# Retention and ELU feed-forward on one core: first batch read in runs of four tokens, heads on partition halves, chunks of 256 tokens, opening reordered

## The chip, the cores and the metric

The kernel runs on one core of one Trainium2 chip. The metric is the device time of one execution in microseconds. Three runs of the kernel before took 302.07, 301.1 and 301.15 us, so its median is 301.15.

## The reference

For each of 8 batches and 8 heads, with 576 tokens and a head size of 64, the scores are weighted with a power of the distance and multiplied with v. There is no softmax. The result, with the heads side by side, is the input of a two-layer network with ELU between the layers.

```python
scores = q @ k.T / sqrt(64)
gamma  = 1 - 2 ** (-5 - h)                       # one per head
ret    = (scores * where(i >= j, gamma ** (i - j), 0)) @ v
x      = ret, as [8 * 576 tokens, 8 heads * 64]
out    = elu(x @ w_in) @ w_out                   # w_in 512 x 2048, w_out 2048 x 512
```

All arrays in HBM are float32; the kernel multiplies in bfloat16. The power splits into a factor on q and a factor on k (`gamma ** i` and `gamma ** -j`), so decay costs one scaling of q and one of k.

## The kernel before

**Items.** The 512 leading tokens of a batch are cut into four *items*: two stretches T of 256 tokens, times two groups w of four heads (L346 to L355). The last 64 tokens of the batches are two tail items at the end. An item goes through these steps:

- `load_main` (L381): three DMAs, q, k and v of the item, 256 KB each. A partition holds two neighbouring tokens of four heads, so a run in HBM is two tokens long, 512 bytes, and 128 partitions take the 256 tokens. The SP queue issues them in the order q, k, v of item 0, of item 1, and so on.
- `scaled` (L469): q and k times their factors, to bfloat16, on VectorE or GpSimd, 128x256 at a time; `cast_v` (L507): v to bfloat16 on ScalarE, VectorE or GpSimd.
- `turn_pe` (L517): TensorE turns q and k; the results are copied from PSUM to `qkT`.
- `do_scores` (L625), `mask_step` (L833): scores of k and q in chunks of 128 tokens (64 partitions, two tokens each), 16 matmuls of 64x128, then one multiplication 128x1024 with the causal mask.
- `do_state` (L722), `after_state` (L738): the product of k and v of each chunk, summed to the running states `mid` and `end`, and laid out by `block` as the block-diagonal tiles `s_mid`, `s_end`. The second chunk of an item and all later ones need a state.
- `do_inter`, `do_values` (L658, L689), `put_x` (L892): q times state plus masked scores times v, copied to `xt`, the input of the network.

The first four items, which are the first batch, go through `early` and `early_out` (L996, L1009): everything by itself, as nothing else is there to do. Later items are woven into the network in `stretch` (L939). From item 12 on (`FAR`) an item has another layout.

**The network.** `ffn1` (L1026) multiplies a block of `xt` with an eighth or sixteenth of w_in, ScalarE takes the exponential, ScalarE or VectorE the positive part, VectorE joins the two; `ffn2` (L1073) multiplies with w_out. The first two blocks are 256 tokens wide, the two halves of the first batch. The weights come in eight pieces of 512 KB after the cast to bfloat16 (1 MB in HBM), issued from GpSimd's queue (`load_w_in`, `load_w_out`, L450, L460).

**What sets the order.** All steps are given to a planner (`Plan`, L37 to L191) as operations with a cost per engine, dependencies, a rank and the buffers they take. It simulates the engines and DMA queues, and at each step gives the free engine the ready operation of lowest rank. The instructions are then issued in the order that comes out (L1203 to L1224), and each engine takes its own in that order. `FROM` (L208) holds the times, in the planner's clock, from which the weight pieces may be issued; `HOLD` (L198) ties the load of item 4 to the landing of the first weight piece; `ON` (L209) fixes the engine of some steps; `RANKS` (L199) shifts ranks and is empty. Where the planner leaves TensorE idle in the first 50 us, matmuls on zeros fill the gap (L1213 to L1222), and ten 128x512 ones go ahead of everything (L1143).

Factors and masks are built before the planned part: the positions by `iota` on GpSimd, the exponents on VectorE, the factors by three exponentials on ScalarE (L1147).

Of the kernel before, what the change touches and what calls it, by code (L numbers as in the profile page):

```python
# [36 lines left out]
class Plan:  # L37
# [30 lines left out]
    def run(self, began):  # L68
# [58 lines left out]
        while len(order) < len(self.ops) or any(wire.values()) or events:  # L127
# [53 lines left out]
            for e, h in heads.items():  # L181
                h[1] -= step * rate[e]
                if h[1] < 1e-6:
                    wire[e].pop(0)
                    lanes[e] -= 1
                    heapq.heappush(events, (now + LEAVE, next(count), h[2]))
# [7 lines left out]
ENTER, LEAVE = 1.25, 0.55  # L194


LEAD = 64
HOLD = {4: "wi0"}  # L198
RANKS = {}  # L199
# [8 lines left out]
FROM = (8.96, 10.28, 13.13, 15.23, 17.0, 17.0, 17.44, 17.82)  # L208
ON = {'mid1': 'DVE', 'be2': 'DVE', 'md_1_0': 'ACT', 'xc1_2': 'DVE', 'cv0': 'DVE', 'md_1_1': 'ACT', 'cq12': 'DVE'}  # L209
DIRECT = True  # L210
# [5 lines left out]
TWO = False  # L216
# [6 lines left out]
FREE = ("f", "e", "g", "ot")  # L223
# [4 lines left out]
    "rqk": 7, "rv": 6, "qkn": 5, "vn": 6, "qkT": 5, "pt": 3,  # L228
    "rqt": 2, "rvt": 2, "qkt": 2, "vt": 4, "qkTt": 8,
    "xt": 3, "g": 28, "e": 4, "ot": 5, "mid": 6, "end": 4, "s_mid": 8, "s_end": 18,  # L230
# [4 lines left out]
def kernel(  # L235
# [44 lines left out]
    lgt = const.tile([P, H], FP32, name="lgt")  # L280
    for h in range(H):
        nc.vector.memset(lgt[:, h : h + 1], lg[h])
    pos_i = const.tile([P, NU], I32, name="pos_i")
    nc.gpsimd.iota(pos_i[:, :FT].rearrange("p (t e) -> p t e", e=2), pattern=[[2 * P, 2], [1, 2]], base=-MID,
                   channel_multiplier=2)
    nc.gpsimd.iota(pos_i[:ST, FT:], pattern=[[0, 1]], base=FT * P - MID, channel_multiplier=1)
    nc.gpsimd.iota(pos_i[ST:, FT:], pattern=[[0, 1]], base=MID - FT * P, channel_multiplier=-1)
    pos = const.tile([P, NU], FP32, name="pos")
    nc.vector.tensor_copy(pos, pos_i)
# [4 lines left out]
    bt = const.tile([P, 1], FP32, name="bt")  # L294
    nc.vector.memset(bt[:ST], math.log(scale))
    nc.vector.memset(bt[ST:], 0.0)
    expo = const.tile([P, NU, H], FP32, name="expo")
    nc.vector.tensor_tensor(
        expo,
        pos.unsqueeze(2).to_broadcast([P, NU, H]),  # L300
        lgt.unsqueeze(1).to_broadcast([P, NU, H]),
        ALU.mult,
    )
    gq = const.tile([P, NU, H], FP32, name="gq")
# [7 lines left out]

    mask = const.tile([P, 2, 2, C], BF16, name="mask")
    nc.vector.memset(mask, 1.0)
    for c in range(2):
        m = mask[c * C : (c + 1) * C]
        nc.gpsimd.affine_select(out=m, in_=m, compare_op=ALU.is_ge, fill=0.0, base=0,
                                pattern=[[-1, 2], [1, 2], [2, C]], channel_multiplier=-2)
    mask_t = const.tile([P, ST], BF16, name="mask_t")
    nc.vector.memset(mask_t, 1.0)  # L320
# [3 lines left out]
    nc.vector.memset(diag[D:, 1:], 1.0)  # L324

# [45 lines left out]
    for n, it in enumerate(items):  # L371
        it.n = n
        it.early = n < FT
        it.far = n >= FAR and not it.tail
        it.xt = xt_of(it.blk)
        it.rank = n * 4 - 64 if it.early else base[it.blk] - LEAD + (
            16 * it.t if it.tail else 6 * it.w + (SPREAD * it.T if width[it.blk] > TB else 0))
# [3 lines left out]
    def load_main(it, srcs="qkv"):  # L381
        n = it.n
        if not hasattr(it, "ld"):
            it.ld = {}
        for s in srcs:
# [3 lines left out]
            away = (s, n) in AWAY  # L389

# [59 lines left out]
    def load_w_in(n0, n1, after):  # L450
        c = slice(n0 * 512, n1 * 512)

        def emit(op):
            pin(nc.gpsimd.dma_start(w_in_sb[:, :, c], moe_w_in[:, c].rearrange("(j p) n -> p j n", p=P)))  # L454

        op = add(f"wi{n0}", {"POOL": 0.8}, [], emit, -1000, dma=(2.62 * (n1 - n0), 32 * (n1 - n0), 4.9), after=after)
        for n in range(n0, n1):
            w_in_ld[n] = op

    def load_w_out(n, after):  # L460
        def emit(op):
            pin(nc.gpsimd.dma_start(w_out_sb[:, 4 * n : 4 * n + 4],
                                    moe_w_out[n * 512 : (n + 1) * 512, :].rearrange("(f p) n -> p f n", p=P)))

        w_out_ld[n] = add(f"wo{n}", {"POOL": 0.8}, [], emit, -1000, dma=(2.62, 32, 4.9), after=after)

    def scaled(it, i, e, cost):  # L469
        n = it.n  # L470
        key, raw = ("qkn", n), ("rq" + "qk"[i], n)
# [3 lines left out]
        def emit(op):  # L475
            pin(alu[op.eng].tensor_tensor(tiles[key][:, i, e], tiles[raw][:, :, e], g, ALU.mult))  # L476
# [4 lines left out]
        ready = [it.ld["qk"[i], e], far_ready[0]] if it.far else [it.ld["qk"[i]]]  # L481
# [25 lines left out]
    def cast_v(it, cost):  # L507
        n = it.n

        def emit(op):  # L510
            pin(copy[op.eng](tiles["vn", n], tiles["rv", n]))  # L511

        ready = [it.ld["v", 0], it.ld["v", 1]] if it.far else [it.ld["v"]]
        it.cv = add(f"cv{n}", cost, ready, emit, it.rank, take=[T("vn", ("vn", n), [P, 4, 2, D], BF16)],
                    use=[("rv", n)])
# [52 lines left out]
    def prepare_tail(it):  # L568
# [3 lines left out]
        for m in range(2):  # L572
            for j in range(2):
                parts = []
                for h in range(2):
                    hs = slice(h * 4, h * 4 + 4)

                    def emit(op, m=m, j=j, hs=hs):
# [4 lines left out]
                                     [it.ld[0, m, j], it.ld[1, m, j]], emit, it.rank,  # L583
# [74 lines left out]
    def do_inter(it, xkey, o=0):  # L658
        n = it.n
        if it.tail:  # L660
            for m in range(2):
                for j in range(2):
                    for hp in range(HP):
                        s = tiles["s_end", 4 * it.t + 2 * m + j, 1, hp // 2]
                        o = (m * HP + hp) * ST
                        acc((xkey, j), 0, 2, tiles[xkey, j][:, o : o + ST], s[:, hp % 2],
                            tiles["qkTt", n, m, j][:, hp, :ST])
# [12 lines left out]
        for c in range(2):  # L680
            if it.T + c == 0:
                continue
            for name in ("s_end", "s_mid") if c and it.two else ("s_mid",) if c else ("s_end",):
# [54 lines left out]
    def after_state(it, st, views, bank_keys):  # L738
# [24 lines left out]
        def block(src, key, name, dep):  # L763
# [7 lines left out]
            return add(name, {"POOL": 0.62, "DVE": (0.42, 0.4 if it.early else 1.5)}, [dep], emit, it.rank + 3,  # L771
                       take=[T(key[0], key, [P, 2, P], BF16)], use=[src])

        it.two = TWO and it.early and it.T == 1
        if it.two or (DIRECT and it.early and it.T == 0):
            key = ("s_mid", it.b, it.T, it.w)

            def emit_bm(op):
                pin(nc.vector.tensor_tensor(
                    tiles[key].rearrange("p h (j d) -> p h j d", j=2),  # L780
                    st_ap(0).unsqueeze(2).to_broadcast([P, 2, 2, D]),
                    diag.unsqueeze(1).unsqueeze(3).to_broadcast([P, 2, 2, D]), ALU.mult,
                ))

            it.bm = add(f"bm{n}", {"DVE": 0.43}, [st], emit_bm, it.rank + 1, take=[T("s_mid", key, [P, 2, P], BF16)],
                        use=[views[0][0]], banks=[bank_keys[0]])
        else:
            it.bm = block(("mid", n), ("s_mid", it.b, it.T, it.w), f"bm{n}", mid)
# [44 lines left out]
    def mask_step(it, sc):  # L833
# [24 lines left out]
        it.mask = add(f"mask{n}", {"DVE": 0.69 if it.far and it.two_of is None else 1.22}, [sc], emit, it.rank + 1,  # L858
# [57 lines left out]
    def cost_of(it, parts):  # L916
# [3 lines left out]
        if "i" in parts:  # L920
            t += 0.056 * (16 if it.tail else 6 if it.two else 4 if it.T else 2)
# [73 lines left out]

    def early(it):  # L996
        n = it.n
# [11 lines left out]
    def early_out(it):  # L1009
        n = it.n  # L1010
# [109 lines left out]

    far_ready = [add("far_i", {"POOL": 0.2}, [], emit_far_i, 0)]
# [4 lines left out]
    for it in items:  # L1126
# [8 lines left out]
    def emit_mask_t(op):  # L1135
        for c in range(2):
            m = mask_t[c * ST : (c + 1) * ST]
            pin(nc.gpsimd.affine_select(out=m, in_=m, compare_op=ALU.is_ge, fill=0.0, base=0, pattern=[[1, ST]],
# [4 lines left out]
    def emit_warm(op):  # L1143
        for _ in range(10):
            mm(tiles["warm"], zero[:, :P], zero, start=True, stop=True)

    def emit_factors(op):  # L1147
        pin(nc.scalar.activation(gq[:, :FT], expo[:, :FT], AF.Exp, bias=bq))
        pin(nc.scalar.activation(gk, expo[:, :FT], AF.Exp, bias=bk, scale=-1.0))
        pin(nc.scalar.activation(gq[:, FT], expo[:, FT], AF.Exp, bias=bt))  # L1150

    add("factors", {"ACT": 0.8}, [], emit_factors, -10 ** 6).at = 2.8
    add("warm", {"PE": 3.0}, [], emit_warm, -10 ** 6, take=[T("f", "warm", [P, 512], FP32)])
# [17 lines left out]
    for i, blk in enumerate(seq):  # L1171
# [3 lines left out]
        rank = base[blk] + width[blk] // 16 + 1  # L1175
# [18 lines left out]
    for n, t in enumerate(FROM):  # L1194
        named[f"{'wi' if n < 4 else 'wo'}{n % 4}"].at = t
        if n % 4:
            named[f"{'wi' if n < 4 else 'wo'}{n % 4}"].turn.append(named[f"{'wi' if n < 4 else 'wo'}{n % 4 - 1}"])
    named["wo0"].turn.append(named["wi3"])
    for name, e in ON.items():
        named[name].cost = {e: named[name].cost[e]}  # L1200
    for name, shift in RANKS.items():
        named[name].rank += shift
# [6 lines left out]
    for op in order:  # L1209
        for cls, key, shape, dt in op.take:  # L1210
            pool = psum if cls in ("f", "sc") else sbuf
            tiles[key] = pool.tile(shape, dt, name=cls, tag=f"{cls}{op.slot[key]}")
        if op.eng == "PE":  # L1213
            gap = op.start - last if op.start < 50 and op.take else 0.0
            if gap > 0:
                spot = tiles[op.take[0][1]]
                for n in range(int(gap * 0.8 / 0.056)):
                    if op.name.startswith("T"):
                        pin(nc.tensor.transpose(spot[:, n % 4], zero[:, :P], ident))
                    else:  # L1220
                        mm((spot if len(spot.shape) == 2 else spot[:, 0])[:, :P], zero[:, :P], zero[:, :P],
                           start=True, stop=True)  # L1222
# [35 lines left out]
```

## Time and profile before

| | us |
|---|---|
| median of three runs | 301.15 |
| the profiled execution | 301.8 |
| its span, first to last instruction | 300.1 |
| TensorE busy in the span | 291.5 |
| ScalarE, VectorE, GpSimd busy | 188.2, 172.3, 164.4 |
| first matmul on weights starts | 19.06 |
| twelve loads of the first batch, first and last landing | 3.72, 15.95 |
| eight weight pieces, first and last landing | 18.00, 40.06 |

The profile is of one execution; its span leaves out what lies around the first and last instruction, here 1.7 us. The granted clock of TensorE is 1.0 over the whole span. In the lists below, PE is TensorE's matmul, PEld its weight load, ACT is ScalarE, DVE VectorE, POOL GpSimd, and SP the engine that issues most DMAs. In a timeline a row has its start, its length, the engine, the line of the kernel, the operation, the tile written and the tiles read, and in brackets how long the engine was idle before and for whom it waited. In a table by windows a row has the stretch, its length, the busy time and number of instructions of PE, PEld, DVE, ACT and POOL, the granted clock, the share of the DMA engines' time and the rate in GB/s.

### The profile page before, as it was taken

To read this page: it belongs to the slowest core of one execution; us is meant where nothing else is said; L and a number is where in the kernel's file an instruction comes from. 1 tells how busy PE (TensorE), PEld (TensorE's weight loads), DVE (VectorE), ACT (ScalarE), POOL (GpSimd) and SP (SyncE) were. 2 spreads that over 40 slices of the span, in tenths; PEclk is the share of its full clock that TensorE was granted. 3 is DMA by queue.
4 is the path that set the end of the run, shared out by engine and by line. 5 is a ranking of instruction groups with operands and counts; after the bars stand their busy time and mean duration, and the time that the engine had idled before them with its cause. 6 is when DMAs were issued, how large, how long until landed. Compare 5 with 4: busy or idle time off the path is not lost.

```text
span 300.1 us, 8496 instructions
## 1 busy us (share of the span) xinstructions
PE 291.5 (97%) x3367; PEld 169.5 (56%) x3402; DVE 172.3 (57%) x312; ACT 188.2 (63%) x365; POOL 164.4 (55%) x292
## 2 busy tenths in 40 slices
PE   8899999999999999999999999999999999999996
PEld 4678746768767764545544554554545444444444
DVE  4888934948865537696843675646442474334300
ACT  2439724838766656786776667676764686777611
POOL 5790389984988849598794888579330000000000
DMA  6999999999998998999999999976761101011132
GB/s 201 272 207 210 226 292 316 231 260 184 179 238 183 217 205 193 219 191 212 192 224 165 173 231 208 186 176 106 175 142 72 35 0 38 35 35 37 35 106 70
DMA packets 135607, 50.10 MB, mean 167 GB/s; under 512 B 108176, under 2 KB 131088, under 8 KB 135568
## 3 DMA queue, kind: packets, MB, share of 16 engines
q1 hardware_dynamic: 131344, 45.37, 71.0%
q0 software_dynamic: 4224, 4.19, 8.4%
q8 instruction: 26, 0.43, 0.6%
q14 instruction: 13, 0.11, 0.1%
HBM read 36.70 MB, written 9.44 MB: 154 GB/s over the span
## 4 chain that ended last, share of the span: by engine, by line
PE 92%; DMA 2%; SPq 2%; issue 1%; POOL 1%; DVE 0%; ACT 0%; ACTq 0%
PE f L269 89%; PE sc L269 3%; DMA rqk<-in_q_dram 2%; SPq L405 2%; POOL qkn L476 1%; PE f L524 1%; POOL w_in_sb L454 0%; DVE xt L907 0%; ACT ot L1094 0%; ACTq L1094 0%
## 5 line engine op out<-in xcount | busy, mean ns | idle before, releaser
L1060 DVE SCALAR_TENSOR_TENSOR g<-e,f 128x512 bf16<-128x512 f32 x144 | 96.3, 685 | 79.3 <-ACT f L1053 78.7
L269 PE MATMUL f<-w_out_sb,g 128*128 128x512 bf16 (+2 forms) x582 | 136.9, 367 | 2.7 <-issue 1.9
L269 PE MATMUL f<-xt,w_in_sb 128*128 128x256 bf16 (+1 forms) x759 | 138.8, 325 | 0.6 <-DVE xt L907 0.2
L1045 ACT ACTIVATE e<-f 128x512 f32<-128x512 f32 x144 | 85.4, 596 | 48.0 <-PE f L269 41.6
L269 PEld LDWEIGHTS <-w_in_sb 128*128 128x128 bf16 x768 | 74.1, 98 | 53.2 <-DVE xt L907 0.5
L269 PEld LDWEIGHTS <-g 128*128 128x128 bf16 x608 | 56.7, 98 | 58.3
L1053 ACT ACTIVATE f<-f 128x512 f32<-128x512 f32 x122 | 72.2, 593 | 0.0
L818 POOL TENSOR_TENSOR s_mid<-mid,diag 128x256 bf16<-128x256 f32 x60 | 35.6, 613 | 12.9 <-DVE mid L807 7.9
L1094 ACT COPY ot<-f 128x512 f32<-128x512 f32 (+2 forms) x38 | 21.4, 566 | 22.6 <-PE f L269 22.6
L476 POOL TENSOR_TENSOR qkn<-rqk,far_q 128x256 bf16<-128x256 f32 x40 | 23.8, 613 | 5.5 <-DMA rqk<-in_q_dram 5.4
L476 POOL TENSOR_TENSOR qkn<-rqk,far_k 128x256 bf16<-128x256 f32 x40 | 23.9, 613 | 0.4 <-DMA rqk<-in_k_dram 0.2
L511 POOL CAST vn<-rv 128x512 bf16<-128x512 f32 x28 | 17.0, 610 | 7.3 <-DMA rv<-in_v_dram 7.3
L476 POOL TENSOR_TENSOR qkn<-rqk,gq 128x256 bf16<-128x256 f32 x21 | 13.1, 635 | 12.1 <-DMA rqk<-in_q_dram 12.1
L907 ACT CAST xt<-f 128x256 bf16<-128x256 f32 x24 | 9.2, 425 | 14.1 <-PE f L269 14.1
L851 DVE TENSOR_TENSOR pt<-sc,mask 128x1024 bf16<-128x1024 f32 x12 | 14.6, 1219 | 4.3 <-PE sc L269 4.2
L845 DVE TENSOR_TENSOR pt<-sc,mask_t 128x1024 bf16<-128x1024 f32 (+1 forms) x12 | 12.5, 1042 | 5.7 <-PE sc L269 4.2
L1055 DVE TENSOR_SCALAR f<-f 128x512 f32<-128x512 f32 x22 | 15.2, 695 | 0.9 <-ACT e L1045 0.6
L579 POOL TENSOR_TENSOR qkt<-rqt,gq 128x256 bf16<-128x256 f32 x16 | 9.5, 613 | 10.6 <-DMA rqt<-in_k_dram 10.6
L883 ACT CAST xt<-f 128x512 bf16<-128x512 f32 x16 | 8.6, 589 | 10.2 <-PE f L269 9.5
L476 POOL TENSOR_TENSOR qkn<-rqk,gk 128x256 bf16<-128x256 f32 x22 | 13.3, 621 | 2.4 <-DMA rqk<-in_k_dram 2.4
L818 POOL TENSOR_TENSOR s_end<-end,diag 128x256 bf16<-128x256 f32 x20 | 12.3, 613 | 0.4 <-DVE end L807 0.3
L807 DVE TENSOR_TENSOR mid<-f,mid 128x256 f32<-128x256 f32 (+1 forms) x24 | 9.1, 380 | 2.5
(81 smaller groups left out, 170.7 us busy)
## 6 DMA issues: line engine op xcount, KB each, us to landing
out_dram<-ot SPq DMA_DIRECT2D x30, 256.0 KB, 3.0
rqk<-in_q_dram SPq DMA_DIRECT2D x40, 128.0 KB, 3.4
rqk<-in_k_dram SPq DMA_DIRECT2D x40, 128.0 KB, 3.3
rv<-in_v_dram SPq DMA_DIRECT2D x40, 128.0 KB, 3.1
rqk<-in_q_dram SPq DMA_DIRECT2D x12, 256.0 KB, 5.8
rqk<-in_k_dram SPq DMA_DIRECT2D x12, 256.0 KB, 5.4
rv<-in_v_dram SPq DMA_DIRECT2D x12, 256.0 KB, 6.9
w_in_sb<-in_moe_w_in_dram POOLq DMA_DIRECT2D x4, 512.0 KB, 8.8
```

The lines of the kernel that those rows point to most:

```text
L269: pin(nc.tensor.matmul(*a, **kw))
L476: pin(alu[op.eng].tensor_tensor(tiles[key][:, i, e], tiles[raw][:, :, e], g, ALU.mult))
L511: pin(copy[op.eng](tiles["vn", n], tiles["rv", n]))
L579: pin(alu[op.eng].tensor_tensor(tiles["qkt", n, m, j][:, hs], tiles["rqt", n, m, j][:, hs], g[:, hs], ALU.mult))
L818: pin(alu[op.eng].tensor_tensor(tiles[out].rearrange("p h (j d) -> p h j d", j=2), tiles[key][:, i].unsqueeze(2).to_broadcast([P, 2, 2, D] ...
L845: pin(nc.vector.tensor_tensor(tiles[it.pt].rearrange("p i h n -> p (i h n)")[:, : 2 * w * C].rearrange("p (i x n) -> p i x n", i=2, n=C), ...
L851: pin(nc.vector.tensor_tensor(tiles["pt", n].rearrange("p i h n -> p (i h) n"), tiles[it.sc].rearrange("p i (h n) -> p (i h) n", h=2), mas ...
L1045: pin(nc.scalar.activation(tiles[ekey], tiles[hkey], AF.Exp))
L1053: pin(nc.scalar.activation(ph, ph, AF.Relu))
L1055: pin(nc.vector.tensor_scalar_max(ph, ph, 0.0))
L1060: pin(nc.vector.scalar_tensor_tensor(tiles[gkey], tiles[ekey], -1.0, tiles[hkey], ALU.add, ALU.min))
L1094: pin(copy[op.eng](tiles[okey][:, :cols], tiles[pkey][:, :cols]))
```

## The change

The first batch gets a path of its own; all later items compute what they did. The diff is cut to the core.

**Loads.** A tensor of 256 tokens and all eight heads is read into one tile by two DMAs, of heads 0 to 3 into partitions 0 to 63 and of heads 4 to 7 into partitions 64 to 127. A partition holds four neighbouring tokens, so a run is 1 KB. There are again twelve DMAs of 256 KB, in the order q, k of tokens 0 to 255, q, k of tokens 256 to 511, v of 0 to 255, v of 256 to 511. An item is now two heads of each half. The four tiles of q and k lie in the place of w_out.

```diff
+            if it.early:
+                raw = ("r8" + s, it.T)
+                for g in range(2):
+                    def emit_quad(op, src=src, raw=raw, g=g):
+                        pin(nc.sync.dma_start(
+                            tiles[raw][g * ST : (g + 1) * ST],
+                            src[it.b, 4 * g : 4 * g + 4, 2 * P * it.T : 2 * P * (it.T + 1), :].rearrange(
+                                "h (p e) d -> p h (e d)", e=4)))
+SEQ = 'q0 k0 q2 k2 v0 v2'
+    for word in SEQ.split():
+        load_main(items[int(word[1])], word[0])
...
+            if cls == "r8" and op.slot[key] < 4:
+                n = op.slot[key] * 4
+                tiles[key] = w_out_sb[:, n : n + 4].bitcast(FP32)...
```

**Chunks of 256 tokens.** `quad` takes the place of `early` and `early_out` for the first four items. The scores of all 256 tokens are computed in two halves of eight matmuls of 64x256, into four banks; the mask is four multiplications 128x512 per item instead of one of 128x1024. There is no state inside a stretch. The value step has 16 matmuls of 64x256, with 16 of 64x64 that build the state in the same bank; for tokens 256 to 511 the latter are done anew for both stretches (32), and two matmuls of 128x256 bring in the state of the first. One copy per item goes to `xt`, one step (`be`) lays out the state. The accumulator of the value step takes the one slot of the class `sc`, so the next item's value step waits for both copies.

```diff
+            sc = add(f"sc{n}_{half}", {"PE": 0.33}, it.turned, emit_sc, it.rank + half, use=[("qkT", n)])
...
+        xv = add(f"iv{n}", {"PE": 0.85 + 0.33 * len(olds)}, [*it.masks, it.cv] + [u.be for u in olds], emit_x, it.rank + 3,
+                 take=[T("sc", xkey, [P, 2, 512], FP32)],
```

**Constants.** The factors and the mask of the first batch are new and small, and are built first. Those of the later items (`near_l`, `near_i`, `near_x`, `near_f`, `mask_n`) become planned operations, and the later scalings and masks wait for them.

**The order.** Costs in the planner change (`QUAD_LD`, `PIECE`), landings in a stretch of its clock get 1.5 us more (`LAG`), eight warm-up matmuls stand for ten, and the fillers use 128x512 matmuls where a gap is long. The load of item 4 is tied to the last w_in piece. `RANKS` and `ON` get long lists, and the second product of the first two blocks a lower rank.

```diff
-HOLD = {4: "wi0"}
-RANKS = {}
+HOLD = {4: 'wi3'}
+RANKS = {'T(5, 0)': 8, 'iv2': -2, 'xc_1': -2, ...}
-FROM = (8.96, 10.28, 13.13, 15.23, 17.0, 17.0, 17.44, 17.82)
+FROM = (5.3, 4.0, 11.5, 8.4, 4.0, 20.1, 7.4, 17.9)
+QUAD_LD = 0.67
+F2_RANK = -16
```

What comes out, by engine, in the opening:

- SP: the twelve loads, then the loads of item 4 on.
- POOL: masks and memsets, one scaling of the first q, three iotas, w_in pieces 0 and 1, eight scalings, w_in pieces 2 and 3, w_out piece 0, the later constants, the other w_out pieces.
- DVE: seven scalings, the later exponents, one copy of turned q and k, then the masks one after another, between them a copy of turned k, one positive part and one copy to `xt`.
- ACT: the factors, three copies of turned q and k, the later factors, a copy, the casts of v of items 0 and 1, a copy, the copy to `xt` of item 0, the cast of v of item 2, the state of item 0 (two copies), the cast of v of item 3, a copy, the copy to `xt` and the state of item 1, then the exponentials.
- PE: warm-up, turns and scores of items 0 and 1, the turns of item 2, the value step of item 0, the scores of item 2, the turns of item 3, the value step of item 1, the scores of item 3, one first product, the value step of item 2, three first products, the value step of item 3, and from there products.

## The prediction

> **What bounds the kernel now.** The head of the page comes first.
>
> ```profile
> span 300.1 us, 8496 instructions
> ## 1 busy us (share of the span) xinstructions
> PE 291.5 (97%) x3367; PEld 169.5 (56%) x3402; DVE 172.3 (57%) x312; ACT 188.2 (63%) x365; POOL 164.4 (55%) x292
> ```
>
> TensorE works nearly all the time. Next is its timeline, to see where it does not.
>
> ```profile
> 14.77 0.56 PE L524 MATMUL f<-ident,qkn 128*128 128x128 bf16 x4 [1.00 <-DVE end L757]
> ...
> 19.06 1.05 PE L269 MATMUL f<-xt,w_in_sb 128*128 128x256 bf16 x8
> ...
> 20.61 1.38 PE L269 MATMUL f<-xt,w_in_sb 128*128 128x256 bf16 x11
> 22.19 8.03 PE L269 MATMUL f<-xt,w_in_sb 128*128 128x256 bf16 x72 [0.21 <-DVE xt L907]
> ```
>
> From 22.19 on it runs through; no later wait in this view is over 0.2 us. So the time is the opening plus a fixed amount of TensorE work. A matmul of the first FFN product costs 0.11 us (72 in 8.03), and 19 of them are done before 22.19, so the FFN starts in effect at 22.19 - 19 x 0.11 = **20.1 us**. This net start is what I follow: one microsecond on it is one on the time. The chain of waits for the first 25 us says what sets it.
>
> ```profile
> 6.33 0.67 SPq L405
> 7.00 0.04 issue
> 7.04 7.02 DMA rqk<-in_q_dram
> 14.06 0.07 issue
> 14.13 0.85 POOL qkn L476
> ...
> 18.39 3.28 PE f L269 x57
> ```
>
> The opening is a chain of loads: the fourth q, issued at 7.04, lands at 14.06. By the trace's landing records the twelve 256-KB loads land at 3.72, 4.55, 6.31 and then every 0.9 us to 11.81; the last three at 14.06, 14.86 and 15.95. So the question is what the new loads do. Three kinds of transfer stand side by side in the table by windows; the last two columns are the DMA engines' share and GB/s.
>
> ```profile
> 8.00:12.00 4.00, 3.89 (x96) 3.18 (x94) 4.00 (x10) 1.72 (x5) 3.96 (x7) 1.00 1.17 292
> 26.00:31.00 5.00, 5.00 (x48) 4.47 (x47) 4.45 (x8) 4.80 (x10) 0.69 (x2) 1.00 1.19 214
> 278.40:279.80 1.40, 1.40 (x9) 0.62 (x7) 0.69 (x1) 0.76 (x3) 0.00 (x0) 1.00 0.83 186
> 288.30:289.10 0.80, 0.80 (x6) 0.35 (x4) 0.00 (x0) 0.00 (x0) 0.00 (x0) 1.00 0.86 328
> ```
>
> The first is the old loads, 128 partitions, runs of 512 B. The second is loads against weight pieces. The third is 256 KB of output stored as two halves of 64 partitions, the fourth the same bytes in one store of 128: 186 against 328 GB/s, with runs of 2 KB in both. In the packet records a packet of the halves takes 153 ns at the median, one of the whole store 85.
>
> **The change, step by step. 1. The loads.** Twelve loads of 256 KB stay, but each now has 64 partitions and runs of 1 KB, in the order q, k of tokens 0-255, q, k of 256-511, then both v. No row shows a 1-KB load or a load of 256 KB on 64 partitions, so I bound it. From below: eight packets of 84 ns per engine, 0.67 us, the packet time of the whole store; 1 KB between the rows of 512 B (28 ns) and 2 KB (84) would be 46 ns x 16 = 0.74. From above: the halves of the store, 1.41 us for 256 KB with start and end, or 8 x 153 ns = 1.22 in a row of loads. I take 1.22, for the row with the same partitions is the nearest, and keep 0.67 to 1.41. The two halves of a tensor follow each other on the same queue, as the halved stores do.
>
> The Trainium skill has a rule on this: SBUF — State Buffer says in its section "Door 1: The DMA port swizzle" that a transfer on partitions 0-63 reaches half of the 16 ports, and in "Can I just issue two DMAs to hit both halves?" that two, one on each half, gain 6% over one. Its 196 GB/s for 64 partitions would make 1.34 us of a half-load (an estimate from that page) and the sum below 1.0 us longer; the 186 of the trace's stores agrees with it, but no run here shows it for loads.
>
> With data from 2.0 (first window above 100 GB/s) and landing 0.75 after the last byte (3.72 = 2.0 + 0.9 + 0.8; 4.55 likewise), q of the first half lands at 2.0 + 2 x 1.22 + 0.75 = 5.2, against 3.72 for half as much data before.
>
> **2. The weights join.** On POOL the first w_in piece now stands behind one scaling (0.85, as at 14.13) that waits for this q, and three iotas (0.13 each): issued at 5.2 + 0.85 + 0.4 = 6.45, the second right behind. Before, issue was at 9.08, and the rate fell from 292 to 245 GB/s at 13.0, 4 us later. So weights join at 10.45, when (10.45 - 2.0)/1.22 = 6.9 half-loads are in. In the stretch 26-31 loads and weights pass packet for packet: load and weight landings both come every 3.65 us (30.17, 33.82, 37.47; 29.04, 32.75, 36.34), with 512 packets each. A half-load has 256, so 1.83 us. The two pieces last 7.3 us, to 17.75; four half-loads pass. k of tokens 256-511 (8th) ends at 12.4, lands at 13.15; v of 0-255 (10th) 16.05 and 16.8; the rest alone, 1.07 x 1.22: the last v lands at **19.8**, against 15.95.
>
> **3. What stands behind the casts of v.** ACT takes its work in order. After the change it is: cast v (items 0, 1), a copy of the transposed k, xc_0, cast v (item 2), two state copies, cast v (item 3), a copy of transposed q, xc_1. The starts of ACT's rows give what one costs in a queue:
>
> ```profile
> 9.19 0.58 ACT L530 COPY qkT<-f 128x512 bf16<-128x512 bf16 x1 [1.13 <-PE f L524]
> 9.67 0.62 ACT L511 CAST vn<-rv 128x512 bf16<-128x512 f32 x1
> 10.19 0.45 ACT L907 CAST xt<-f 128x256 bf16<-128x256 f32 x1
> ```
>
> 0.5 each; a 128x128 copy 0.27, so two 0.5. From 16.8: cast, then the first value product 17.45 to 18.3, xc_0 to 19.1, idle to 19.8, cast to 20.3, states to 20.85 (they free the one accumulator, so the second value product runs 20.95 to 21.75), cast 21.4, copy 21.9, xc_1 to 22.6. TensorE does item 3's scores meanwhile and starts the first FFN product at **22.75**, three matmul groups behind a chain that before had none of v in it.
>
> **4. TensorE's own work.** Sixteen 64x64 matmuls take 0.25 us to the next start, sixteen of 64x128 0.35; 256 columns then 0.35 + 0.2 = 0.55. A value step of tokens 256-511 is 0.55, two rounds of states 0.5, and two 128x256 at 0.11: 1.27. Both of these still come after 22.75, so the net start is 22.75 + 2.54 = **25.3**, and the change costs 25.3 - 20.1 = **5.2 us**.
>
> **5. What I cost at nothing.** Masks: 16 of 128x512, half of the 1.22 of 128x1024, 9.8 us on DVE instead of 4.9; with the last v at 19.8 they lie in the wait for it, and if v comes early they are late next (rival 2). The constants of the later batches move to POOL and ACT in the opening, under a microsecond each, covered by the same wait; the new waits on them are met 10 us before use. Eight warm-up matmuls for ten, fewer fillers: idle time either way. Raw q and k lie in w_out's place, so those pieces wait for scalings over by 17; wo0 follows w_in by 10 us, before its first use. Loads of item 4 held for wi3 instead of wi0, and the shifts of rank and engine later: after 22 us TensorE alone binds; 0.3 either way.
>
> **How it could go.** *Forecast, halves at half rate*: 301.15 + 5.2 = 306.4 us. The sum is made on a profiled execution of span 300.1, which itself took 301.8, 0.65 above the median; it would take 307.0. With 1.41 the same steps give 21.3 for the last v and +6.7, 307.9. For it: the third row above, and weights that join before the loads are done.
>
> *Rival 1, halves that overlap in part*: before, the sixteen parts of a load land up to 1.3 us apart, so engines out of step would fill both halves at once. With 1.0 us a half-load the same steps land v at 18.1, +3.5: 304.7. Against it: the two halves of a store show no such gain (186 GB/s over both).
>
> *Rival 2, no loss from halves, and faster*: it decides below about 0.8 us a half-load. At 0.67 weights join at 9.35 with 11 of 12 in, the last v lands at 12.0, and DVE binds: first mask at 8.0 (k at 5.4, four scalings 1.4, turn, copy, scores 1.2), 16 x 0.61 and 1.7 of others to 19.5, last value product to 21.0 with 3.5 us of FFN already done: 17.5, so -2.6, 298.5. At 0.74 v lands at 13.7, -0.9, 300.2; at 0.82 at 15.3, +0.7, 301.8. For it: half the packets, the old loads at 292 GB/s were below the 328 that longer runs show.
>
> *Late parts*: q at 14.06 was held by one of sixteen parts 1.5 us behind the others (12.51); if this hits the last v, each case is up to 1.5 later. TensorE would wait over 3 us for v; its first ten 128x512 matmuls took 0.43 each against 0.22 later. A fall back to that pace after the wait costs up to 1.5; I add neither, but the top of the range has them.
>
> **Numbers.** Forecast 0.52, rival 1 0.15, rival 2 0.33 (of it 0.25 clearly faster, 0.07 no change, 0.01 slower). A measurement here tells 0.3% (0.9 us) from no change: faster 0.25, same 0.07, slower 0.68. Likeliest case 304.9 to 308.4; the range that leaves out 2 in 10, 298.8 to 308.4.
>
> **What would show it.** Right: in the first 10 us windows near 215 GB/s where 292 stood; DVE's or POOL's first scaling after 5 us; ACT idle before a cast of v up to about 20; the FFN stream from about 23. Wrong: windows above 330 GB/s, the last v before 14, or DVE with no gap between masks: then rival 2.

## The result, and the profile after

The kernel after took **308.77 us** (median of four runs, 307.85 to 309.81) against 301.12 for the kernel before: 1.025 times as long, 95% interval 1.021 to 1.029, or 7.65 us more. The forecast was 306.4, so the direction is right and the size 2.4 us short. The range ended at 308.4 and missed the time by 0.4 us.

The profiled execution took 309.8, some 1.0 above the median; its span is 308.1, 8.0 more than the profiled one of before. First the head of its page.

```profile
span 308.1 us, 8508 instructions
## 1 busy us (share of the span) xinstructions
PE 297.9 (97%) x3379; PEld 171.3 (56%) x3379; DVE 175.2 (57%) x308; ACT 197.5 (64%) x382; POOL 160.5 (52%) x299
```

The shares look as before. The difference is in the first 32 us, and the table by windows has it (granted clock, share of the DMA engines' time and GB/s are the last three columns).

```profile
5.00:10.00 5.00, 3.57 (x30) 2.50 (x29) 3.23 (x9) 1.73 (x4) 2.80 (x6) 1.00 1.11 216
10.00:15.00 5.00, 3.50 (x59) 2.30 (x56) 4.10 (x7) 1.28 (x5) 3.12 (x6) 1.00 1.16 219
15.00:20.00 5.00, 3.65 (x65) 2.77 (x64) 2.87 (x5) 2.83 (x4) 4.88 (x9) 0.74 1.19 238
20.00:25.00 5.00, 3.12 (x55) 2.40 (x56) 1.45 (x3) 3.90 (x8) 3.10 (x9) 0.50 1.24 206
25.00:30.00 5.00, 5.00 (x76) 3.84 (x75) 3.65 (x6) 1.93 (x5) 0.00 (x0) 0.74 1.21 212
30.00:35.00 5.00, 5.00 (x88) 4.28 (x86) 3.67 (x9) 4.82 (x11) 0.61 (x1) 1.00 1.20 215
```

Two things are to be seen. Where the loads stand alone, up to 13.8, when the first packet of a weight piece is moved, they move at 216 to 219 GB/s (292 before), with the DMA engines busy all the time. And the granted clock, 1.0 throughout before, is at half from 17.4 to 27.6 us by the clock records. The chain of waits in order of time (start, length, what) names what it hangs on:

```profile
8.22 12.47 DMA r<-in_v_dram
...
20.77 0.62 ACT vn L552
21.39 0.16 ACT blocks L1109
...
21.88 1.28 PE sc L275 x20
23.16 3.47 PE f L275 x29
```

The last load, v of tokens 256 to 511, lands at 20.70 by the landing records; the casts and state copies follow on ScalarE, then TensorE. TensorE's timeline shows what the clock does to the steps:

```profile
19.36 0.63 PE L568 MATMUL f<-ident,qkn 128*128 128x128 bf16 x4
21.88 1.07 PE L275 MATMUL sc<-pt,vn 64*64 64x256 bf16 x16 [1.88 <-ACT blocks L1109]
...
23.74 1.07 PE L275 MATMUL f<-qkT 64*64 64x256 bf16 x16
24.74 1.89 PE L275 MATMUL f<-xt,w_in_sb 128*128 128x256 bf16 x8
26.42 0.64 PE L275 MATMUL sc<-qkT,blocks 128*128 128x256 bf16 x2
...
28.10 2.79 PE L275 MATMUL f<-xt,w_in_sb 128*128 128x256 bf16 x24
...
31.86 2.31 PE L275 MATMUL f<-xt,w_in_sb 128*128 128x256 bf16 x19
```

The first product (eight matmuls) takes 1.89 here and took 1.05 before. From 31.86 the stream runs through, with 32 products of 0.11 done: the net start is 31.86 - 3.5 = **28.35**, against 20.1 before. That is 8.25 later, and the span is 8.0 longer: nearly all of the loss lies in the opening.

### The profile page after: what moved, and what is told of

The parts are those of the page before. It is cut to its first block, busy times and chain, and to the rows that moved or that the text cites. A ratio compares the mean times of both kernels' runs of the same rounds, so it can differ in the third digit from the quotient of the medians.

```text
span 308.1 us, 8508 instructions
## 1 busy us (share of the span) xinstructions
PE 297.9 (97%) x3379; PEld 171.3 (56%) x3379; DVE 175.2 (57%) x308; ACT 197.5 (64%) x382; POOL 160.5 (52%) x299
## 4 chain that ended last, share of the span: by engine, by line
PE 92%; DMA 4%; SPq 2%; ACT 0%; issue 0%; ACTq 0%
PE f L275 88%; DMA r<-in_v_dram 4%; PE sc L275 4%; SPq L407 2%; PE f L568 0%; ACT vn L552 0%; ACT blocks L1109 0%; ACT ot L1220 0%; ACTq L1220 0%; ACTq L552 0%
## 5 line engine op out<-in xcount | busy, mean ns | idle before, releaser
L275 PE MATMUL f<-w_out_sb,g 128*128 128x512 bf16 (+2 forms) x608 | 143.0, 368 | 0.0
L275 PE MATMUL f<-xt,w_in_sb 128*128 128x256 bf16 (+1 forms) x768 | 142.1, 327 | 0.0
L555 POOL CAST vn<-rv 128x512 bf16<-128x512 f32 x26 | 15.8, 610 | 8.2 <-DMA rv<-in_v_dram 8.1
L516 POOL TENSOR_TENSOR qkn<-rqk,gq 128x256 bf16<-128x256 f32 x14 | 8.5, 613 | 19.1 <-DMA rqk<-in_q_dram 19.1
L1055 DVE TENSOR_TENSOR pt<-f,quad_m 128x512 bf16<-128x512 f32 x16 | 10.1, 685 | 6.2 <-PE sc L275 5.5
L939 ACT CAST xt<-f 128x256 bf16<-128x256 f32 x21 | 7.8, 423 | 6.2 <-PE f L275 6.2
L883 DVE TENSOR_TENSOR pt<-sc,mask 128x1024 bf16<-128x1024 f32 x8 | 9.8, 1220 | 2.3 <-PE sc L275 2.3
```

What stands on the lines that cost most here:

```text
L275: pin(nc.tensor.matmul(*a, **kw))
L883: pin(nc.vector.tensor_tensor(tiles["pt", n].rearrange("p i h n -> p (i h) n"), tiles[it.sc].rearrange("p i (h n) -> p (i h) n", h=2), mas ...
L1055: pin(nc.vector.tensor_tensor(tiles[ptk][:, i].rearrange("p k n -> p (k n)").rearrange("p (k n) -> p k n", k=2), tiles[key].rearrange("p ( ...
```

## The experiments

**1. The loads alone.** A kernel with six forms of load, each twelve times 256 KB.

```diff
+    def half(n, b):       # 64 partitions, 4 heads, runs of 1 KB
+        pin(nc.sync.dma_start(raw[n][64 * g : 64 * g + 64]..., x))
+    def half_two(n, b):   # the same, two queues
+        pin((nc.scalar if g else nc.sync).dma_start(...))
+    def whole(n, b):      # 128 partitions, 2 heads of 512 tokens, runs of 1 KB
```

> Only loads, none of the reference's computation: six groups of twelve loads of 256 KB, each group alone on the DMA engines. In order: the form before (128 partitions, runs of 512 B, one queue); the form after (halves of 64 partitions, runs of 1 KB, one queue); the same halves, the two of a pair on two queues; halves with runs of 512 B; 128 partitions with runs of 1 KB; 128 partitions, 1 KB, as pairs of 128 KB on two queues. Theory, the partitions of one transfer limit it: 0.9 us a load in the first group, 1.2 in the second and fourth whatever the run, 0.9 or less in the fifth and sixth, and 0.6 to 0.9 a load in the third, because both halves are then in flight. Rival, the run or the shape of the source limits it: 1.2 in every group with runs of 1 KB, 0.9 in both with 512 B. Rival, two queues gain nothing (a rule in the Trainium skill, page SBUF — State Buffer, gives 6%): third group 1.1 to 1.2.

The table by windows of this kernel, one row within each group, in the order of the groups (the engines are VectorE and GpSimd only; GB/s last):

```profile
4.00:12.00 8.00, 6.03 (x7) 0.00 (x0) 1.00 1.08 293
17.00:24.00 7.00, 5.94 (x7) 0.00 (x0) 1.00 1.13 234
36.00:43.00 7.00, 4.83 (x6) 0.00 (x0) 1.00 1.15 207
49.00:57.00 8.00, 6.70 (x9) 0.00 (x0) 1.00 1.21 222
58.00:64.00 6.00, 5.19 (x6) 0.00 (x0) 1.00 1.06 326
80.00:120.00 40.00, 6.38 (x7) 0.00 (x0) 1.00 0.14 48
```

64 partitions give 207 to 234 GB/s, with runs of 1 KB or 512 B; 128 partitions 293 with 512 B and 326 with 1 KB. So the partitions of one transfer set the pace, and the run length alone would have made the loads faster: about 0.72 us a load, against 0.89. (This is one execution, and the groups run into each other a little at their ends.)

The third row needs care. ScalarE's halves went out from 19.65 us on, beside the second group, and by the packet records its queue moved nothing between 35 and 40 us: the row is for the most part SP's halves alone. In the stretch before it both queues had packets in every microsecond:

```profile
22.00:34.00 12.00, 5.80 (x7) 0.00 (x0) 1.00 1.05 216
```

At 216 GB/s, against 234 for one queue, nothing is gained, and the loads of both queues landed one behind the other, 1.1 to 1.3 us apart; the 0.6 to 0.9 that the theory gave for this group was wrong. The rule that the prediction names from SBUF — State Buffer of the Trainium skill, that two transfers on the two halves hardly beat one, agrees. The pairs were not always on opposite halves, so it is not a clean trial of that rule. The last row of the table is a trap of its own, told under experiment 2.

**2. All partitions, same places.** Four loads of 128 KB for each tensor instead of two of 256 KB, each over both halves.

```diff
+                        x = src[...].rearrange("(r h) (p e) d -> h r p (e d)", r=2, e=4)
+                        for h in (2 * g, 2 * g + 1):
+                            pin((nc.scalar if h % 2 else nc.sync).dma_start(tiles[raw][:, h], x[h]))
```

> Kernel after, with the same bytes to the same places, but each tensor read by four loads of 128 KB that span all 128 partitions, on SP's and ScalarE's queues in turn. Theory, the pace of the half loads sets the end: last v 3 to 5 us earlier than 20.70 (16 to 17.5), first FFN product 3 to 5 us before 24.74, time 303.5 to 306. Rival, the new order behind v (casts, copies, value steps on one engine) sets it: loads earlier, but time within 1 us of 308.8.

It took 383.4 us, and tells nothing of the theory. In its windows and in the last group above (pairs of 128 KB over 128 partitions) the loads move at 46 to 48 GB/s with a DMA share of 0.14, two of sixteen engines. The source's outermost dimension is r, of size 2. The Trainium skill has the rule in DMA: Bandwidth & Descriptors, section "Why a DMA increments its semaphore by 16 and not by 1": the slowest dimension decides among how many engines a transfer is split. Both runs agree with it.

**3. All partitions, other rows.** One load of 128 partitions that takes 512 tokens of two heads: as many bytes, as many DMAs, all later instructions the same.

```diff
-                            tiles[raw][g * ST : (g + 1) * ST],
-                            src[it.b, 4 * g : 4 * g + 4, 2 * P * it.T : 2 * P * (it.T + 1), :]...
+                            tiles[raw][:, 2 * g : 2 * g + 2],
+                            src[it.b, 2 * o : 2 * o + 2, : 4 * P, :].rearrange("h (p e) d -> p h (e d)", e=4)))
```

> Kernel after, but each load of the first batch is one of 128 partitions: 512 tokens of two heads instead of 256 tokens of four, as many bytes in runs of 1 KB. The rows of q, k and v then stand in other places than the steps behind them assume, so the first batch's output is not the reference's; every instruction behind the loads is the same. Theory, the halves set the end: 0.72 us a load (fifth group of the run of loads alone) instead of 1.21, last v at 2.0 + 12 x 0.72 + 0.75 = 11.4 instead of 20.7, TensorE's last value step before the stream of products near 24 instead of 31.9, the clock at 1.0, and 300 to 302.5 us. Rival, the new order (masks on one engine, casts and copies on another, value steps of 1.27) sets the end: 304 to 307 with v equally early.

304.15 us, 1.007 of before (1.003 to 1.012): the partitions of the loads are worth 1.8% or 5.4 us of the 7.5 that the change costs. The first eight loads land by 9.80, 0.7 to 0.8 apart but for one step of 1.8; but the weights, issued 1.9 us earlier as q lands earlier, hold the last v until 17.48 (11.4 was expected). So the time stays above the theory's 302.5. It lies in the rival's range, 304 to 307, but that had the last v equally early, and it was not: the run doesn't tell the two apart, and experiment 5 has to. Its seven executions spread from 302.27 to 306.44.

**4. Weights later.** The order is left, but for two pieces.

```diff
+    for name, spot in (('wi0', 'cq12'), ('wi1', 'wi0')):
+        order.remove(named[name])
+        order.insert(order.index(named[spot]) + 1, named[name])
```

> Kernel after, with the first two w_in pieces issued two scalings later on GpSimd, behind the wait for the q of tokens 256 to 511 (about 11.9 instead of 7.03). Theory, sharing with the weights costs the last v 2.9 us (20.70 against 17.8 at 1.21 us a half-load): last v near 17.8, first product 1.5 to 2.5 us earlier, time 306 to 307.5. Rival, the weights' own landing takes its place (19.84 becomes 22 to 24): no gain, 308 to 310.

305.9 us, 1.013 of before (1.008 to 1.019): 3.5 us better by the ratios. The last v lands at 18.22 instead of 20.70, and wi0 at 20.73 is early enough for a first product that now starts at 21.34. That is just beyond the better end of what the theory gave in time, and well beyond it at the first product: 3.4 us earlier, where 1.5 to 2.5 was said. The granted clock is a part of this. It falls here too, but earlier, and is back before the value steps that wait for v:

```profile
10.00:15.00 5.00, 4.75 (x58) 3.50 (x56) 4.25 (x9) 1.65 (x5) 3.96 (x6) 0.51 1.14 218
```

From 15 us on it is 1.0. In the profiled executions the net start is 4.2 us earlier (24.1): 2.5 go with the earlier v, and the rest is about what the slow stretch costs after (experiment 6), which is missing here.

**5. Both.** Experiment 3 with the two pieces one scaling later (`('wi0', 'cq02')`).

> span128 with the first two w_in pieces behind one more scaling on GpSimd (issued near 8.4 instead of 5.1; the first batch's output is not the reference's, as in span128). Theory, what is left in span128 over before (2.4 us) is the last v at 17.5, held by the weights: v by 13, and 301 to 302.5, level with before. Rival, the value steps and masks of the new chunks are what is left: v by 13, but 303.5 to 304.5.

301.77 us, 1.000 of before (0.998 to 1.002). The last v lands at 13.15. The second window of its table shows the rate of the loads, 337 GB/s where after has 216, and TensorE's timeline where the stream begins:

```profile
5.00:10.00 5.00, 3.98 (x61) 2.92 (x59) 4.53 (x12) 2.38 (x6) 2.69 (x5) 1.00 1.01 337
```

```profile
22.80 0.63 PE L275 MATMUL sc<-pt,vn 64*64 64x256 bf16 x16
23.27 0.42 PE L275 MATMUL sc<-vn,qkn 64*64 64x64 bf16 x32
23.62 5.47 PE L275 MATMUL f<-xt,w_in_sb 128*128 128x256 bf16 x48
```

23.62 less the same 32 products is 20.1, the kernel before to the tenth. Four kernels now make a table of two causes, as ratio to before. "As in after" means the same place in the order: with 128 partitions the q ahead of the weights lands earlier, and wi0 goes out at 5.11 instead of 7.03. "Later" is two scalings in the first row (12.16) and one in the second (7.99).

| | weights as in after | weights later |
|---|---|---|
| loads on 64 partitions | 1.025 | 1.013 |
| loads on 128 partitions | 1.007 | 1.000 |

The partitions are worth 1.3 to 1.8% (4.0 to 5.4 us), the place of the weights 0.7 to 1.2% (2.1 to 3.5 us); by the intervals each of these four is sure only to some 2 us, and each holds what the clock does in the two kernels compared. With both gone nothing of the loss is left. That doesn't make the rest of the change free. The loads of span_late are faster than those of before (337 GB/s for 292), and its last v lands 2.8 us earlier (13.15 for 15.95), yet it is no faster; rival 2 of the prediction had counted on 0.9 to 2.6 us from a v at 13.7 to 12.0. Either the chunks of 256 tokens, with their masks and value steps in the new order, eat up what the earlier v brings, or so early a v is no longer what the stream waits for. No run here separates the two.

**6. The clock.** Matmuls on zeros for 0.7, 1.0 and 1.7 us more, ahead of three steps that wait.

```diff
+EXTRA = {'T(2, 1)': 0.7, 'iv0': 1.0, 'T(3, 1)': 1.7}
-            if gap > 0:
+            fill = gap * 0.8 + EXTRA.get(op.name, 0.0)
+            if fill > 0:
```

> Kernel after, with matmuls on zeros for 0.7, 1.0 and 1.7 us more (at full clock) ahead of the last turn of item 2, the first value step and the last turn of item 3, in the waits. Theory, the waits of TensorE halve its clock and that is about 2 us of the loss: the granted clock near 1.0 in the windows 20 to 30, the first product 0.9 us instead of 1.89, time 306.3 to 307.3. Rival, the pace has another cause or the fillers only push the turns back: 308.5 to 309.5.

307.83 us, 1.019 of before (1.015 to 1.024; after 1.021 to 1.029): between the theory's range and the rival's, in neither. The cause is seen in the trace, in the same stretch as above:

```profile
20.00:25.00 5.00, 3.76 (x79) 2.91 (x80) 2.95 (x5) 3.98 (x9) 3.12 (x9) 1.00 1.24 206
```

```profile
21.40 0.63 PE L276 MATMUL sc<-pt,vn 64*64 64x256 bf16 x16 [0.76 <-ACT blocks L1110]
...
23.86 0.93 PE L276 MATMUL f<-xt,w_in_sb 128*128 128x256 bf16 x7 [0.36 <-ACT xt L1096]
...
29.51 4.71 PE L276 MATMUL f<-xt,w_in_sb 128*128 128x256 bf16 x41
```

Its last v lands at 20.22, but the clock stays at 1.0 and the stream runs from 29.51 instead of 31.86. Between the profiled executions that is 2.35 us (span 305.6, 2.5 less); 0.48 of it is the earlier v (second value step 21.40 for 21.88), the other 1.9 the clock. Between the medians it is 0.94, and the intervals overlap: the profiled execution of after was 1.0 above its median, that of this kernel 0.5 below. How long the clock is down differs from run to run (mean clock 0.978 to 0.989 in the four of after, 0.994 to 1.0 in the four here), and the time doesn't follow it strictly: the lowest, 0.978, is that of after's fastest execution. The slower matmuls and their cure are plain in the trace; the size, 0.9 to 1.9 us, is not settled closer. With experiment 4 and these fillers together:

> weights_late and fill together, without the plain copy and its eight half stores. If those stores cost the loss in combo (TensorE waited 2.2 us for turned q and k at 68 to 74 us, behind a queue with twice the stores): 305 to 306, as weights_late, with at most 0.5 us more from the clock. If it was the fillers: 307 to 308.

306.46, 1.016 (1.013 to 1.019), against 1.013 without the fillers: between the two ranges, and no gain. In experiment 4 the clock was back by itself before it mattered, and the fillers put the second value step at 20.60 instead of 19.53.

**7. The interleaved copy.** ScalarE's rows behind v, in after:

```profile
15.60 1.14 ACT L552 CAST vn<-r 128x512 bf16<-128x512 f32 x2 [2.77 <-DMA r<-in_v_dram]
16.65 0.58 ACT L574 COPY qkT<-f 128x512 bf16<-128x512 bf16 x1
17.12 1.31 ACT L1095 CAST xt<-sc 128x512 bf16<-128x512 f32 x1
20.77 0.62 ACT L552 CAST vn<-r 128x512 bf16<-128x512 f32 x1 [2.34 <-DMA r<-in_v_dram]
21.30 0.53 ACT L1109 CAST blocks<-sc 64x128 bf16<-64x128 f32 x2
...
23.20 1.30 ACT L1095 CAST xt<-sc 128x512 bf16<-128x512 f32 x1
```

The order is the one predicted, but the copy to xt takes 1.31 where 0.6 was taken. The edit writes it in the accumulator's order and lets the stores sort the rows, eight of them instead of four.

```diff
-            pin(copy[op.eng](dst, tiles[xkey][:, :, : 2 * P].rearrange("p h (e t) -> p h e t", e=4)))
+            pin(copy[op.eng](dst, tiles[xkey][:, :, : 2 * P]))
...
+                        for e in range(2):
+                            pin(nc.sync.dma_start(rows[2 * it + e], tiles[okey][e * ST : (e + 1) * ST, :cols]))
```

> Kernel after, with the copy to xt writing whole rows in the order of the accumulator, and the output rows of the first batch put in order by the stores instead. Theory, the interleaved copy (1.31 us, against 0.6 in the prediction) costs 0.7 on the chain to the first product through the second copy: that copy near 0.6, time 307.7 to 308.3. Rival, the copy is slow for its size, not for its pattern: still 1.2 to 1.3, same time as after.

308.26 us, 1.022 (1.017 to 1.026). That is in the range of the theory too, but within the noise of after, so the trace has to decide. The copy does take 0.58, so the pattern makes it slow, not the size. But the first product starts at 24.75 as before the edit: TensorE's scores at half clock (23.74 to 24.74 above) end no sooner. The 0.7 lies beside them. At full clock it doesn't: in experiment 6 TensorE waits 0.36 for the copy in the middle of its first product (the row at 23.86).

The same edit with those of experiments 4 and 6 (combo):

> The edits of weights_late, fill and xplain together. If the three terms add (2.9, 0.9, 0.7): 304 to 304.8. If they cover each other (the clock loss is there only while v is late): 305.2 to 306.

308.24, as much as after and above both ranges, though its last value step ends at 28.05, 3.8 us before that of after. (Its profiled execution, 309.64, is 1.4 above the median.) Part of the gain is given back later:

```profile
PE sc L276 <- DMA qkT<-qkn: 2.2, 2, 1.2
PE f L276 <- issue: 1.4, 9, 0.2
PE f L276 <- POOL s_mid L851: 0.7, 2, 0.3
```

TensorE waits for q and k turned by DMA (columns: total, times, longest), on SP's queue behind the doubled stores. Without those (late_fill, above) this wait is not there. But xplain has the same doubled stores and no such wait either, so the stores alone don't make it; it came where all three edits met, and why stays open.

The edit with experiment 3 and the fillers:

> span128 with the edits of fill and xplain (output not the reference's for the first batch, as in span128). Theory: once v is early neither the clock nor the ScalarE queue is on the path, so within 0.7 us of span128. Rival, the masks on VectorE bind and fillers or copies still count: 1 to 2 us below span128.

304.01, 1.007 (1.005 to 1.010): as span128. So in that kernel fillers and copy together bring nothing that can be measured, as the theory said. But v wasn't early as the theory's wording has it (17.06, against 17.48 in span128), and these stores are doubled as well.

And experiment 5 with the copy in the accumulator's order, the stores left as they were:

> span_late with the copy to xt in the order of the accumulator, and the stores as they were (the first batch's output rows then stand in another order too, besides what span128 changes). In span_late the second value step waits 0.61 for ScalarE behind a first copy of 1.31, and the first product 0.36 for the second copy. Theory, with v early these copies are on the path: both at 0.6, these two waits gone, the last value step before the stream of products 0.7 to 1.1 earlier than 23.6, time 300.6 to 301.2. Rival, the masks on VectorE are next behind: the copies faster, the last value step within 0.3 of 23.6, time as span_late.

301.76, 1.000 (0.998 to 1.002). The copies take 0.59 and both waits are gone, yet the stream is reached only 0.4 earlier (23.23), between what the theory (0.7 to 1.1) and the rival (up to 0.3) gave, and the time is the same, as the rival said. Its reason, masks on VectorE that come next, is not shown: after 12 us none of TensorE's waits in this trace is put down to VectorE. No kernel here beats the kernel before.

**8. Half loads in the kernel before.**

```diff
+                if it.early:
+                    pin(nc.sync.dma_start(dst[:ST], x[:ST]))
+                    pin(nc.sync.dma_start(dst[ST:], x[ST:]))
+                    return
```

> Kernel before, nothing changed but the twelve loads of the first batch: each is two DMAs of 64 partitions, one after the other on the same queue, into the same tile. Theory, partitions halved means pace halved, whatever the kernel around: 1.15 to 1.2 us per 256 KB instead of 0.9, q of the fourth item 3 to 4 us later than 14.06, time 303.5 to 306. Rival, it takes the new layout and order to make the loads slow: within 1 us of before. A guard: if the queue's issues (0.5 to 0.7 each, now 24) set the pace instead, the packets of 512 B stay near 28 ns instead of 45.

311.36 us, 1.032 (1.028 to 1.036), beyond both ranges, but the guard decides: the packets of 512 B stay at 27 ns and the DMA share between 5 and 10 us is 0.70, so the engines were not full. Twenty-four issues of 0.66 us set the pace, and the weights then took their turn among the late ones. It shows that twice as many loads of half the size are bad for that kernel, not whether by their number or by their partitions. Left inconclusive.

## Why the prediction was right in sign and short in size

- **What bounds the kernel, and the net start as the measure**: right. Later net start by 8.25 us, longer span by 8.0.
- **Step 1, the loads**: right. 1.22 us for a half-load was predicted, 1.20 measured (landings from 4.54 to 12.91 in seven steps of 1.14 to 1.21). Only the start was off: q of the first half landed at 5.69, not 5.2. The 1.34 worked out from the Trainium skill's 196 GB/s would have been 0.14 too long; the same section of SBUF — State Buffer, "Door 1: The DMA port swizzle", gives 218 GB/s as the limit for long transfers on 64 partitions, and the 216 to 219 of these windows agree with that; the same form of load alone, in experiment 1, ran at 234, 1.12 us a load, which is above that limit, and the measurement decides; why is open. Rival 1 (overlap of halves, 1.0) and rival 2 (no loss) fell with the 216 GB/s of the first window.
- **Step 2, the weights join**: two errors that offset each other. wi0 was issued at 7.03 (6.45), but its first packet came 6.8 us later, at 13.8, not 4. (In before it came 3.2 us after the issue, at 12.30 by the packet records; the prediction took its 4 from the rate.) So v of tokens 0 to 255 landed earlier than said (15.52 for 16.8), and the last v met all of the sharing: fifteen of its sixteen parts landed by 19.58, the last at 20.70. That the 15th came so near the 19.8 predicted is luck: the two errors happened to be of one size.
- **Step 3, ScalarE's queue**: right in order, TensorE waiting for it at 21.88. From the last v to the first product it gave 2.95; it was 4.04. ScalarE's copy to xt was mis-sized (1.31 for 0.6), but here that lay beside other work, TensorE's at half pace: second value step 1.07 for 0.63 in its first part, scores 1.07 for 0.63, fillers 0.72 for 0.45. At full clock the copy is what TensorE waits for instead (experiment 6).
- **Step 4, TensorE's own work**: a value step of tokens 256 to 511 is 1.13 at full clock (30.73 to 31.86), 1.27 predicted. But the first product took 0.8 longer, and the third value step 1.68 instead of 1.13.
- **Step 5, costed at nothing**: held. VectorE waited for TensorE twice between its masks (2.15 and 3.39 us), and no wait of TensorE over 0.2 us comes after the opening.
- **The step that failed is "late parts"**, named in the prediction and added neither to the sum nor fully to the range. Both of its halves came in the same execution: a part of the last v 1.1 us behind the others, and TensorE at half pace. In the profiled execution the miss of 3.05 us on the net start (28.35 for 25.3) is 0.9 from the last v, 1.1 + 0.8 + 0.55 = 2.45 from the steps behind it (from v to the first product, that product, the third value step), and -0.3 from the shorter value steps. Experiment 6 takes 1.9 of the 2.45 away, so that is the clock's. Most of the half microsecond that is left there is another term: with the clock at 1.0, TensorE waits 0.36 for the mis-sized copy of step 3, which the half pace hides in after. The prediction had allowed 1.5 for each of the two and put neither into the forecast, although its own sum held a wait of TensorE of over 3 us; the top of the range, 2.0 above the forecast, has no room for both. Nor is it quite the mechanism that was named: the clock fell at 17.39, before the longest wait (1.88, up to 21.88); the two waits just ahead of it were of 0.86 and 1.10. Between the medians the clock is worth only 0.9, so the size of this term is not settled.
- What the prediction did not say is that the order of the weights is a cause of its own, worth 2.1 to 3.5 us by the table (each sure only to some 2 us, and with the clock's share in it). It had it inside step 2 as part of the landing of v, but never asked what the kernel would do with the pieces issued later.

## What to carry to other kernels

Price a load by the partitions of one transfer before its run length: here 64 partitions cost 1.1 to 1.2 us per 256 KB and 128 partitions 0.72 to 0.89, and a second queue brought nothing. Where a sum contains waits of TensorE of a microsecond or more, the slower matmuls behind them belong in the sum, not in the margin. And what shares the wire with the last load on the path should be issued so that it joins behind it, as long as its own first use allows.

## What the runs showed of the chip that was not expected

- A load whose outermost dimension has size two ran at 48 GB/s, with 1 KB per packet and 46 ns a packet: two engines' worth.
- A copy 128x512 from PSUM that writes every fourth element of a row took 1.31 us on ScalarE and on VectorE, the same copy in rows 0.58 and 0.68.
- Packets of 512 B to 64 partitions took 45 ns in a full queue (fourth group of the loads alone) and 27 ns in one that was not full (experiment 8).
- TensorE's granted clock fell to half in after without a long wait before it: up to then no wait between its matmuls was over 1.10 us. It was back to 1.0 after 10.2 us, with TensorE busy from 24.74 on.
- One of the sixteen parts of the last v of after came 1.1 us behind the other fifteen, some time after an instruction fetch of 16 KB (17.0 to 18.0 us). Xplain, fill and span_all, with such a fetch in the 3 us or so before that landing, have gaps of 0.6 to 1.3; weights_late, combo and late_fill, where the fetch comes as v lands or later, 0.1 at most. Span128 (0.3 with a fetch before) and span_late (0.55 without one) don't fit. That the fetch is the cause was not tried.
